# Upward products as 64-row halves on both row tiles, two units at a time, in a fused attention and channel-mix kernel

## The chip, the cores and the metric

The kernel runs on one core of one Trainium2 chip. The metric is the device time of one execution in microseconds (us); each time below is of this one core.

## What is computed

Two operators, one after the other, on x of shape 4 x 12608 x 128 (batch, tokens, channels), all in float32:

```python
# 1: attention through 32 inducing points; m = 32, C = 128, scale = C ** -0.5
def mab(q, kv):
    s = scale * (q @ kv.transpose(0, 2, 1)); s = s - s.max(-1, keepdims=True)
    a = np.exp(s); a /= a.sum(-1, keepdims=True) + 1e-09
    return a @ kv
h = mab(I, x)          # 32 x 128 per batch
x = mab(x, h)          # every token attends to the 32 rows of h
# 2: channel mix with the token before; d_ff = 1024
xk = mu_k * x + (1 - mu_k) * x_prev
xr = mu_r * x + (1 - mu_r) * x_prev
k = np.maximum(xk @ w_k, 0); v = k * k @ w_v
out = sigmoid(xr @ w_r) * v
```

The second attention's result is a product of weights `a` (tokens x 32) with `h`. So xk @ w_k is a[t] @ (h * mu_k @ w_k) + a[t-1] @ (h * (1 - mu_k) @ w_k): the kernel never forms x again, it multiplies the 32 weights of a token and of the token before with two small matrices W that it makes once per batch.

## The kernel before

**Tiling.** A batch has 25 groups of tokens: 24 of 512 (G) and a last one of 320. A block is four groups, so a batch has seven blocks, the last with the 320 tokens alone. d_ff is 1024 = 8 chunks of 128; a *unit* is one group with two chunks (UC = 2), four units to a group, so 100 units to a batch and 400 in all.

**A unit.** `up` (L774) makes the products of two chunks in PSUM, `square` (L786) has VectorE take the maximum with 0 (L792) and ScalarE square it twice, once rounded to fp32r (kh, L797; in some units VectorE does that, L794) and once in full (L798); GpSimd takes the difference kl (L800). `down` (L803) multiplies kh and kl with the high and low parts of w_v, six matmuls into one PSUM bank, four units after the unit's `up` (LAG = 4). Once in four units `zgate` (L761) makes the gate: two matmuls (L769, L770) and a sigmoid (L772). `gate` and `store` finish a group.

**Split numbers.** A matmul takes fp32r, a rounded float32. So the weights `a` are kept as a high and a low part. The tile R of a group, 128 rows x 513, holds in its four strips of 32 rows high, low, high, low; W[0] (this token, mu_k) and W[1] (the token before) hold in theirs high, high, low, low. One 128-row matmul thus gives all four cross products, and the token before is the same R one column to the left. That makes four 128-row matmuls in an `up`: for each of two chunks W[0] with R[:, 1:w+1] (L780) and W[1] with R[:, 0:w] (L782).

**Where R and W come from.** `stage_b` (L599) makes the weights of a block in steps at due times t to t+9 and `spread` (L663) puts one group a unit, from t+10 on, into R with four DMAs on SP's queue, and one more (`halo`, L589) for the column of the token before. For the first four groups `stage_b_head` (L688) does it with transposes on TensorE and one ScalarE copy (L745). `combine` (L473) makes h and W: scaled copies of h (L515), products with w_k and w_r, high on ScalarE, low on VectorE; for the first batch eight full products L538 with L541 and L544, for the others packs of four in the column strips (L556) and then 24 DMAs (L572) that spread the strips into W.

**The order of the work** is written out by hand: in the loop over units n (from L1017) each engine's queue gets, in this order, `gate` of a group that is done, `up(n)`, `square(n)`, GpSimd's difference, `zgate` if the unit is the second of its group, `store`, `down(n-4)`, and then the events whose due time is n. `stage_a` (first attention of the next batch, L313) and `stage_b` put their steps into this table at due times counted in units, 12 units to a block (SEG), from the offset t = 100 b (plus 4 for the first batch, L996). The engines then run their queues in order and wait for one another by semaphores. `spin` (L889) is a short burst of TensorE work in the head whose results nobody reads.

PSUM has eight banks: ps_a two tiles of two banks (the `up` products), ps_v two, pb_a and pb_b one each. So `up(n)` waits until VectorE has read `up(n-2)`.

Of the kernel before, what the change touches and what calls it, by code (L numbers as in the profile page):

```python
# [8 lines left out]
F32 = mybir.dt.float32  # L9
# [10 lines left out]
def kernel(  # L20
# [24 lines left out]
    LAG = 4  # L45
    UO = 2
# [10 lines left out]
    r_pool = ctx.enter_context(tc.tile_pool(name="r_pool", bufs=10))  # L57
# [415 lines left out]
    def combine(b, at=None, t=0):  # L473
# [18 lines left out]
        def weights():  # L492
# [11 lines left out]
            sw = sm.tile([P, P], F32, name="mk", bufs=1)  # L504
            if ahead:
                nc.vector.tensor_scalar(out=sw, in0=stack_f, scalar1=wt, scalar2=rd,
                                        op0=ALU.mult, op1=ALU.mult)
            else:
                nc.vector.tensor_scalar(out=sw, in0=stack_f, scalar1=rd, scalar2=None, op0=ALU.mult)
            L["sw"] = sw  # L510

        def mixed(*parts):
            for nm, mu in parts:
                h4 = L["h4"][nm] = sm.tile([P, P], F32, name="h4" + nm, bufs=1)
                nc.vector.tensor_scalar(out=h4, in0=L["hp"], scalar1=mu, scalar2=None, op0=ALU.mult)  # L515

        def hfin():
            ps = pb_tile(None if ahead else "b")
            nc.tensor.matmul(out=ps[:, :P], lhsT=S.acc, rhs=L["sw"], start=True, stop=True)
            h = sm.tile([P, P], F32, name="hT")  # L520
            nc.vector.tensor_copy(out=h, in_=ps[:, :P])
            S.hT = h[:, :M]
            L["hp"] = ps[:, :P]
            L["h4"] = {}
            mixed(("k0", muk), ("k1", omuk))
            mixed(("r0", mur), ("r1", omur))
            S.W = [wp.tile([P, WF], F32R, name=f"W{s}") for s in range(2)]

        def wpart(s, c, tile):

            X = {}
            c0, cw, nm, src = ((F, C, f"r{s}", wr_sb) if c is None else
                               (c * G, G, f"k{s}", wk_sb[:, c * G:(c + 1) * G]))
            dst = S.W[s][:, c0:c0 + cw]

            def prod():
                X["ps"] = tile()[:, :cw]
                nc.tensor.matmul(out=X["ps"], lhsT=L["h4"][nm], rhs=src, start=True, stop=True)  # L538

            def high():  # L540
                nc.scalar.copy(out=dst, in_=X["ps"])  # L541

            def low():
                nc.vector.tensor_tensor(out=dst[P // 2:], in0=X["ps"][P // 2:, :],  # L544
                                        in1=dst.bitcast(F32)[P // 2:], op=ALU.subtract)
            return prod, high, low

        def wpack(parts, cw, tags, t):

            X = {}  # L550
            rows = M * len(parts)

            def prod():
                X["ps"] = pb_tile("a")
                for n, (s, nm, c0, src) in enumerate(parts):
                    nc.tensor.matmul(out=X["ps"][M * n:M * (n + 1), :cw], lhsT=L["h4"][nm][:, :M], rhs=src,  # L556
                                     start=True, stop=True)

            def high():
                X["hi"] = st.tile([P, G], F32R, name=tags[0], bufs=tags[2])[:rows, :cw]  # L560
                nc.scalar.copy(out=X["hi"], in_=X["ps"][:rows, :cw])

            def low():
                lo = st.tile([P, G], F32R, name=tags[1], bufs=tags[2])[:rows, :cw]
                hi = X["hi"].bitcast(F32)
                nc.vector.tensor_tensor(out=lo, in0=X["ps"][:rows, :cw], in1=hi, op=ALU.subtract)
                X["hl"] = (hi, lo.bitcast(F32))

            def spread(n):
                s, nm, c0, src = parts[n]  # L570
                for q in range(Q):
                    nc.sync.dma_start(out=S.W[s].bitcast(F32)[M * q:M * (q + 1), c0:c0 + cw],  # L572
                                      in_=X["hl"][q // 2][M * n:M * (n + 1)])
            at(t, prod)
            at(t, high)
            at(t + 1, low)
            for n in range(len(parts)):
                at(t + 1 + n, lambda n=n: spread(n))
# [5 lines left out]
        parts = [(s, f"k{s}", c * G, wk_sb[:, c * G:(c + 1) * G]) for c in range(F // G) for s in range(2)]  # L584
        for n in range(0, len(parts), Q):
            wpack(parts[n:n + Q], G, ("ah", "al", 1), t + 11 + 4 * (n // Q))
        wpack([(s, f"r{s}", F, wr_sb) for s in range(2)], C, ("xs", "xs", 3), t + 13)

    def halo(S, g, far=True):  # L589

        if g == 0:
            nc.vector.memset(S.R[g].bitcast(F32)[:, 0:1], 0.0)
        elif far:
            nc.sync.dma_start(out=S.R[g].bitcast(F32)[:, 0:1], in_=S.R[g - 1].bitcast(F32)[:, G:G + 1])
        else:
            nc.vector.tensor_copy(out=S.R[g][:, 0:1], in_=S.R[g - 1].bitcast(F32)[:, G:G + 1])


    def stage_b(b, j, at, t):  # L599
# [55 lines left out]
        def high():  # L655
            L["ah"] = st.tile([P, G], F32R, name="ah")[:, :w]
            nc.scalar.copy(out=L["ah"], in_=L["aT"])

        def low():
            L["al"] = st.tile([P, G], F32R, name="al")[:, :w]  # L660
            nc.vector.tensor_tensor(out=L["al"], in0=L["aT"], in1=L["ah"].bitcast(F32), op=ALU.subtract)

        def spread(i):  # L663
            src = (L["ah"].bitcast(F32), L["al"].bitcast(F32))
            if full or i == 0:
                S.R[j * Q + i] = r_pool.tile([P, G + 1], F32R, name="R")
                halo(S, j * Q + i)
            R = S.R[j * Q + (i if full else 0)].bitcast(F32)
            o, lo = (0, 0) if full else (offs[i], i * w - offs[i])
            for q in range(Q):  # L670
                nc.sync.dma_start(out=R[M * q:M * (q + 1), 1 + o + lo:1 + o + w],
                                  in_=src[q % 2][M * i:M * (i + 1), lo:w])
# [12 lines left out]
        for i in range(Q):  # L685
            at(t + 10 + i, lambda i=i: spread(i))

    def stage_b_head(gs):  # L688
# [7 lines left out]
        def scores():  # L696
            ps = L["ps"] = pb_tile("b")
            for k, g in enumerate(gs):
# [5 lines left out]
                S.R[g] = r_pool.tile([P, G + 1], F32R, name="R")  # L704

        def diff():
            s2 = L["s2"] = st.tile([P, Q * Q, M], F32, name="s2")[:, :n, :]
# [16 lines left out]
        def place(k):  # L724
            g = gs[k]
            X = {}

            def src():
                return L["s2"][:, k * Q:(k + 1) * Q, :].unsqueeze(2).broadcast_to([P, Q, 2, M])

            def high():
                X["a"] = st.tile([P, G], F32R, name=("ah", "al")[g % 2]) \
                    .rearrange("p (k q m) -> p k q m", k=Q, q=Q)
                nc.scalar.copy(out=X["a"][:, :, 0::2, :], in_=src())

            def low():
# [110 lines left out]
    def halves():  # L847

        for name in ("kh", "kl"):
            for _ in range(4):  # L850
                yield mp.tile([P, UC, G], F32, name=name, bufs=4)
# [228 lines left out]
```

## Time and profile before

| what | value |
|---|---|
| median of 3 runs | 1146.32 us (1145.34 to 1148.07) |
| profiled execution | 1144.99 us, its span 1142.9 us, granted TensorE clock 0.993 |
| busy: PE, DVE, ACT, POOL | 1103.4, 917.7, 971.3, 948.4 us |
| instructions | 17673 |
| DMA | 102.32 MB in 274988 packets |

PE is TensorE's matmuls, PEld its weight loads, DVE VectorE, ACT ScalarE, POOL GpSimd, SP the engine whose queue issues nearly all DMAs. Busy time of PE is a union of spans: matmuls are pipelined, a matmul of 512 columns is drawn about 0.39 us long while the next one starts 0.23 us after it. So pace is read from starts, not from lengths. A row of the timeline gives the start, the time that the merged instructions cover, the engine, the line, tiles and shape (`64*128 64x512` is a stationary operand of 64 rows and 128 columns, and 64 rows x 512 columns that move), and in brackets the idle time before and what ended it.

### The profile page before, as it was taken

The page shows a single profiled execution, that of the slowest core. Times are in us where ns is not written, and L with a number is a line of the kernel's source. Part 1 is how long each engine was busy: PE and PEld are TensorE (multiplying, and loading weights), DVE is VectorE, ACT ScalarE, POOL GpSimd, SP SyncE. Part 2 cuts the span into 40 slices and gives each one's busy share as a digit, 9 for nine tenths or more (in the row PEclk, how much of TensorE's full clock was granted, in tenths as well). Part 3 has the DMA queues.
Part 4 walks back from the last instruction along what each step waited for, and adds up shares of the span by engine and source line. Part 5 has one row for each costly group of instructions (what it writes and reads, how often), then busy time and mean ns, then how long its engine had stood idle before and what let it go on. Part 6 is the DMA issues. An engine that isn't in the chain of part 4 may idle for free.

```text
span 1142.9 us, 17673 instructions
## 1 busy us (share of the span) xinstructions
PE 1103.4 (97%) x5716; PEld 837.4 (73%) x5716; DVE 917.7 (80%) x1294; ACT 971.3 (85%) x1107; POOL 948.4 (83%) x413
## 2 busy tenths in 40 slices
PE   6778999999989999999999999999999999999997
PEld 4456777777777777777877777777778777777886
DVE  5687898987678889897777889898777888887665
ACT  5477889888988888888988988889889988889996
POOL 1157888998887988888889888888888899999996
PEclk9999999999999999999999999999999999999999
DMA  9213444555135455555124455545222233242212
GB/s 275 69 28 91 106 108 111 129 127 108 31 70 119 91 121 124 125 124 124 24 61 87 110 128 120 129 99 124 50 50 61 46 64 59 54 74 56 43 28 34
DMA packets 274988, 102.32 MB, mean 90 GB/s; under 512 B 234288, under 2 KB 249808, under 8 KB 272592
## 3 DMA queue, kind: packets, MB, share of 16 engines
q1 hardware_dynamic: 274560, 101.18, 40.7%
q8 instruction: 45, 0.74, 0.3%
q14 instruction: 47, 0.39, 0.1%
q10 hardware_dynamic: 336, 0.02, 0.0%
HBM read 28.07 MB, written 25.82 MB: 47 GB/s over the span
## 4 chain that ended last, share of the span: by engine, by line
PE 79%; DVE 8%; ACT 7%; issue 3%; SPq 2%; DMA 1%; DVEq 0%; ACTq 0%
PE ps_v L811 40%; PE ps_a L780 15%; PE ps_a L782 13%; DVE k_t L792 3%; PE pb_b L617 2%; PE ps_v L769 2%; PE ps_v L770 2%; PE pb_a L359 2%; ACT kh L797 2%; PE pb_a L428 2%; ACT L772 1%; ACT L634 1%; ACT k_t L798 1%; SPq L93 1%; DVE kh L794 1%
## 5 line engine op out<-in xcount | busy, mean ns | idle before, releaser
L800 POOL TENSOR_TENSOR kl<-k_t,kh 128x1024 fp32r<-128x1024 f32 (+2 forms) x400 | 939.6, 2377 | 154.1 <-ACT k_t L798 136.4
L792 DVE TENSOR_SCALAR k_t<-ps_a 128x1024 f32<-128x1024 f32 (+1 forms) x400 | 480.2, 1201 | 162.1 <-PE ps_a L782 147.0
L798 ACT ACTIVATE k_t<-k_t 128x1024 f32<-128x1024 f32 (+1 forms) x400 | 418.3, 1048 | 46.9 <-DVE kh L794 35.7
L797 ACT ACTIVATE kh<-k_t 128x1024 fp32r<-128x1024 f32 (+1 forms) x352 | 366.0, 1040 | 81.5 <-PE ps_v L811 45.0
L780 PE MATMUL ps_a<-R,W 128*128 128x512 f32 (+1 forms) x800 | 324.5, 406 | 8.9 <-DMA R<-al 4.8
L782 PE MATMUL ps_a<-R,W 128*128 128x512 f32 (+1 forms) x800 | 314.3, 393 | 0.0
L811 PE MATMUL ps_v<-kh,wvh 128*128 128x512 f32 (+1 forms) x800 | 249.8, 393 | 5.3 <-ACT rT L772 4.7
L811 PE MATMUL ps_v<-kh,wvl 128*128 128x512 f32 (+1 forms) x800 | 249.3, 393 | 0.0
L811 PE MATMUL ps_v<-kl,wvh 128*128 128x512 f32 (+1 forms) x800 | 249.1, 392 | 0.1
L780 PEld LDWEIGHTS ps_a<-R,W 128*128 128x128 f32 x800 | 151.4, 189 | 82.9 <-issue 19.9
L811 PEld LDWEIGHTS ps_v<-kh,wvh 128*128 128x128 f32 x800 | 149.4, 189 | 44.0 <-ACT rT L772 10.0
L811 PEld LDWEIGHTS ps_v<-kl,wvh 128*128 128x128 f32 x800 | 150.3, 189 | 34.8 <-POOL kl L800 0.4
L811 PEld LDWEIGHTS ps_v<-kh,wvl 128*128 128x128 f32 x800 | 150.4, 189 | 34.1
L782 PEld LDWEIGHTS ps_a<-R,W 128*128 128x128 f32 x800 | 151.3, 189 | 30.7
L816 DVE TENSOR_TENSOR oT<-ps_v,rT 128x512 f32<-128x512 f32 (+1 forms) x100 | 66.7, 667 | 2.3
L827 DVE STREAM_TRANSPOSE ot<-oT 128x512 f32<-128x512 f32 x96 | 67.2, 700 | 0.0
L794 DVE SCALAR_TENSOR_TENSOR kh<-ps_a,k_t 128x1024 fp32r<-128x1024 f32 x48 | 58.8, 1225 | 5.4 <-DVE k_t L792 0.5
L772 ACT ACTIVATE rT<-ps_v 128x512 f32<-128x512 f32 (+1 forms) x99 | 57.3, 579 | 0.3
L331 DVE STREAM_TRANSPOSE xs<-xb 128x512 f32<-128x512 f32 x72 | 50.0, 694 | 2.5 <-DMA xt<-xs 1.2
L772 ACT ACT_TABLE_LOAD x31 | 39.8, 1283 | 0.5
L769 PE MATMUL ps_v<-R,W 128*128 128x512 f32 (+1 forms) x99 | 39.2, 396 | 0.8 <-DVE oT L816 0.8
L770 PE MATMUL ps_v<-R,W 128*128 128x512 f32 (+1 forms) x99 | 38.9, 393 | 0.0
(196 smaller groups left out, 614.8 us busy)
## 6 DMA issues: line engine op xcount, KB each, us to landing
out_dram<-ot SPq DMA_DIRECT2D x184, 128.0 KB, 3.3
xb<-in_x_dram SPq DMA_DIRECT2D x18, 1024.0 KB, 5.6
xt<-xs SPq DMA_DIRECT2D x288, 64.0 KB, 2.0
R<-ah SPq DMA_DIRECT2D x184, 64.0 KB, 2.0
R<-al SPq DMA_DIRECT2D x184, 64.0 KB, 2.0
kh<-in_x_dram SPq DMA_DIRECT2D x4, 512.0 KB, 7.3
kl<-in_x_dram SPq DMA_DIRECT2D x4, 512.0 KB, 7.5
xb<-in_x_dram SPq DMA_DIRECT2D x8, 256.0 KB, 5.8
```

The lines of the kernel that those rows point to most:

```text
L769: nc.tensor.matmul(out=ps[:, :w], lhsT=S.W[0][:, F:WF], rhs=R[:, 1:w + 1], start=True, stop=False)
L772: nc.scalar.activation(out=self.rT, in_=ps[:, :w], func=AF.Sigmoid)
L780: nc.tensor.matmul(out=ps[:, c, :w], lhsT=S.W[0][:, cs], rhs=R[:, 1:w + 1], start=True, stop=False)
L782: nc.tensor.matmul(out=ps[:, c, :w], lhsT=S.W[1][:, cs], rhs=R[:, 0:w], start=False, stop=True)
L792: nc.vector.tensor_scalar(out=k, in0=self.ps[:, :, :w], scalar1=0.0, scalar2=None, op0=ALU.max)
L794: nc.vector.scalar_tensor_tensor(out=kh, in0=self.ps[:, :, :w], scalar=0.0, in1=k, op0=ALU.max, op1=ALU.mult)
L797: nc.scalar.activation(out=kh, in_=k, func=AF.Square)
L798: nc.scalar.activation(out=k, in_=k, func=AF.Square)
L800: return lambda eng, a, z: eng.tensor_tensor(out=kl[:, :, a:z], in0=k[:, :, a:z], in1=kh.bitcast(F32)[:, :, a:z], op=ALU.subtract)
L811: nc.tensor.matmul(out=self.v, lhsT=wt[:, fc, :], rhs=kk[:, c, :], start=(fc == 0 and n == 0), stop=(fc == FC - 1 and n == 2))
L816: nc.vector.tensor_tensor(out=self.oT, in0=self.v, in1=self.rT, op=ALU.mult)
L827: nc.vector.transpose(out=ot[:, o:o + w], in_=self.oT)
```

## The change

It has these parts:

- `up` keeps the chunks but changes the products (new constants: HP = 64, NR = 5). R now has 64 rows that matter: 0 to 31 the token's weights, 32 to 63 those of the token before, and rows 64 to 127 the same again; its second index says high or low. W[0] (high) and W[1] (low) hold in rows 0 to 63 the even chunks (this token over the token before), in rows 64 to 127 the odd ones. A unit is then three products (W high x R high, W low x R high, W high x R low; low x low is left out), each as two matmuls of 64 rows, one on each row tile of the array, into two PSUM banks.
- `up(n)` and `up(n+1)` are issued one after the other, at even n; both `down`s follow later as before, as whole matmuls of 128 rows.
- `zgate` still has two whole matmuls, now with one matrix Wg of 128 rows against R high and R low.
- W is made by one pack of four products whose strips lie already as W needs them: one ScalarE copy, one VectorE difference, no DMA. Wg likewise.
- R is filled by two DMAs (the token's rows, and the same one column on), a small one for the first column, and two units later by one DMA of 64 rows x 2 x 512 (`double`) that copies rows 0 to 63 to 64 to 127. R has 5 buffers instead of 10, and a fill is due no earlier than the last unit of the group five before.
- The first four groups: eight transposes of 32 columns a group; for group 0 four ScalarE and four VectorE copies, for the others one of each and `double`.
- kh has 5 buffers instead of 4; the first batch's offset in the table of due times is 1 instead of 4.

```diff
-    r_pool = ctx.enter_context(tc.tile_pool(name="r_pool", bufs=10))
+    r_pool = ctx.enter_context(tc.tile_pool(name="r_pool", bufs=NR))
...
         def hfin():
-            nc.tensor.matmul(out=ps[:, :P], lhsT=S.acc, rhs=L["sw"], start=True, stop=True)
+            nc.tensor.matmul(out=ps[:, :M], lhsT=S.acc, rhs=L["sw"], start=True, stop=True)
...
+            h4 = L["h4"] = sm.tile([P, Q, M], F32, name="h4", bufs=1)
+            for n, mu in enumerate((muk, omuk, mur, omur)):
+                nc.vector.tensor_scalar(out=h4[:, n, :], in0=ps[:, :M], scalar1=mu, scalar2=None, op0=ALU.mult)
+            S.W = [wp.tile([P, F // 2], F32R, name=f"W{s}") for s in range(2)]
+            S.Wg = wp.tile([P, C], F32R, name="Wg")
...
             def prod():
                 X["ps"] = tile()[:, :cw]
+                chunks = wk_sb.rearrange("p (c e d) -> p e c d", e=2, d=P)
+                for n in range(Q):
+                    o = X["ps"][M * n:M * (n + 1), :]
+                    if not gate:
+                        o = o.rearrange("m (c d) -> m c d", d=P)
+                    nc.tensor.matmul(out=o, lhsT=L["h4"][:, 2 * gate + n % 2, :],
+                                     rhs=wr_sb if gate else chunks[:, n // 2], start=True, stop=True)
             def high():
+                nc.scalar.copy(out=(S.Wg if gate else S.W[0]), in_=X["ps"])
             def low():
+                hi, lo = (S.Wg, S.Wg) if gate else S.W
+                nc.vector.tensor_tensor(out=lo[rows], in0=X["ps"][rows], in1=hi.bitcast(F32)[rows],
+                                        op=ALU.subtract)
...
+        for gate in range(2):
+            prod, high, low = wpart(gate, lambda: pb_tile("a"))
+            at(t + 11 + 2 * gate, prod)
+            at(t + 11 + 2 * gate, high)
+            at(t + 12 + 2 * gate, low)
...
+    def new_r(S, g, src=None):
+        R = S.R[g] = r_pool.tile([P, 2, G], F32R, name="R")
...
+        nc.sync.dma_start(out=rf[M:HP, :, 0:1], in_=src[:, :, G - 1:G])
+    def double(S, g):
+        rf = S.R[g].bitcast(F32)
+        w = G if g < NG - 1 else TAIL
+        nc.sync.dma_start(out=rf[HP:, :, :w], in_=rf[:HP, :, :w])
+    def fill(rf, src, o, n, width):
+        for s in range(2):
+            m = min(n, width - o - s)
+            nc.sync.dma_start(out=rf[M * s:M * (s + 1), :, o + s:o + s + m], in_=src[:, :, :m])
...
         for i in range(Q):
-            at(t + 10 + i, lambda i=i: spread(i))
+            f = b * NG + j * Q + (i if full else 0)
+            s = max(t + 10 + i, NU * (f - NR) + 3 + (0 if full else i))
+            at(s, lambda i=i: spread(i) if full else spread_tail(i))
+            assert s + 4 <= NU * f, (b, j, i)
+            if full or i == Q - 1:
+                at(s + 2, lambda g=j * Q + i if full else j * Q: double(S, g))
...
+        def put(k, whole):
             g = gs[k]
+            ps = pa.tile([P, 2, G], F32, name="ps_a")
+            for s in range(2):
                 for c in range(Q):
+                    nc.tensor.transpose(out=ps[:M, s, c * P:(c + 1) * P], identity=ident,
+                                        in_=L["a"].bitcast(F32)[:, k * Q + c, s, :])
...
+            if not whole:
+                nc.scalar.copy(out=R[:M], in_=ps[:M])
+                nc.vector.tensor_copy(out=R[M:HP, :, 1:], in_=ps[:M, :, :G - 1])
+                return
...
+            for s in range(2):
+                for r in range(2):
+                    nc.scalar.copy(out=R[HP * r:HP * r + M, s], in_=ps[:M, s])
+                    nc.vector.tensor_copy(out=R[HP * r + M:HP * (r + 1), s, 1:], in_=ps[:M, s, :G - 1])
...
-            for c in range(UC):
-                cs = slice((u * UC + c) * P, (u * UC + c + 1) * P)
-                nc.tensor.matmul(out=ps[:, c, :w], lhsT=S.W[0][:, cs], rhs=R[:, 1:w + 1],
-                                 start=True, stop=False)
-                nc.tensor.matmul(out=ps[:, c, :w], lhsT=S.W[1][:, cs], rhs=R[:, 0:w],
-                                 start=False, stop=True)
+            for n, (a, k) in enumerate(((0, 0), (1, 0), (0, 1))):
+                for r in range(2):
+                    rows = slice(HP * r, HP * (r + 1))
+                    nc.tensor.matmul(out=ps[:, r, :w], lhsT=S.W[a][rows, u * P:(u + 1) * P],
+                                     rhs=R[rows, k, :w], start=(n == 0), stop=(n == 2))
...
-        t = b * UB + (4 if b == 0 else 0)
+        t = b * UB + (1 if b == 0 else 0)
...
-                grp.up(u)
+                if n % 2 == 0:
+                    for g, v in units[n:n + 2]:
+                        g.up(v)
```

More of the change, by code (lines that the diff above doesn't have):

```diff
@@ L45 @@
     LAG = 4
+    HP = P // 2
+    NR = 5
     UO = 2
@@ L546, in wpart @@
             return prod, high, low
[L548 to L578, printed above, removed]
@@ L655, in high, with spread_tail @@
         def high():
-            L["ah"] = st.tile([P, G], F32R, name="ah")[:, :w]
-            nc.scalar.copy(out=L["ah"], in_=L["aT"])
+            if full:
+                L["hl"] = st.tile([P, 2, G], F32R, name="hl", bufs=2)
+            else:
+                L["hl"] = st.tile([P, G], F32R, name="xs", bufs=3)[:, :2 * w].rearrange("p (s t) -> p s t", s=2)
+            nc.scalar.copy(out=L["hl"][:, 0, :], in_=L["aT"])
         def low():
-            L["al"] = st.tile([P, G], F32R, name="al")[:, :w]
-            nc.vector.tensor_tensor(out=L["al"], in0=L["aT"], in1=L["ah"].bitcast(F32), op=ALU.subtract)
+            nc.vector.tensor_tensor(out=L["hl"][:, 1, :], in0=L["aT"], in1=L["hl"].bitcast(F32)[:, 0, :],
+                                    op=ALU.subtract)
         def spread(i):
[L664 to L672, printed above, removed]
+            hl = L["hl"].bitcast(F32)
+            g = j * Q + i
+            src = hl[M * i:M * (i + 1)]
+            rf = new_r(S, g, hl[M * (i - 1):M * i] if i else None)
+            fill(rf, src, 0, G, G)
+        def spread_tail(k):
+            g = j * Q
+            rf = new_r(S, g) if k == 0 else S.R[g].bitcast(F32)
+            lo = k * w - offs[k]
+            fill(rf, L["hl"].bitcast(F32)[M * k:M * (k + 1), :, lo:], k * w, w - lo, TAIL)
         at(t, scores)
@@ L748, in stage_b_head, with high, low @@
-        return scores, diff, expo, norm, [place(k) for k in range(len(gs))]
+        def high():
+            a = L["a"] = st.tile([P, 2, G], F32R, name="hl", bufs=2) \
+                .rearrange("p s t -> p (s t)")[:, :2 * n * M].rearrange("p (k s m) -> p k s m", s=2, m=M)
+            nc.scalar.copy(out=a[:, :, 0, :], in_=L["s2"])
+        def low():
+            nc.vector.tensor_tensor(out=L["a"][:, :, 1, :], in0=L["s2"], in1=L["a"].bitcast(F32)[:, :, 0, :],
+                                    op=ALU.subtract)
@@ L751 @@
+        return scores, diff, expo, norm, high, low, put
     NG = (NBLK - 1) * Q + 1
@@ L768, in zgate @@
                 ps = self.v = pv.tile([P, G], F32, name="ps_v")[:, :w]
-            nc.tensor.matmul(out=ps[:, :w], lhsT=S.W[0][:, F:WF], rhs=R[:, 1:w + 1], start=True, stop=False)
-            nc.tensor.matmul(out=ps[:, :w], lhsT=S.W[1][:, F:WF], rhs=R[:, 0:w], start=False, stop=True)
+            for s in range(2):
+                nc.tensor.matmul(out=ps[:, :w], lhsT=S.Wg, rhs=R[:, s, :w], start=(s == 0), stop=(s == 1))
             self.rT = mp.tile([P, G], F32, name="rT")[:, :w]
```

130 lines of the change are left out of this document (38 added, 92 removed).

## The prediction

> **What bounds the kernel now.** I read the page first: the shares of the engines, the chain of work that ended last, and the costliest groups.
>
> ```profile
> span 1142.9 us, 17673 instructions
> PE 1103.4 (97%) x5716; PEld 837.4 (73%) x5716; DVE 917.7 (80%) x1294; ACT 971.3 (85%) x1107; POOL 948.4 (83%) x413
> PE 79%; DVE 8%; ACT 7%; issue 3%; SPq 2%; DMA 1%; DVEq 0%; ACTq 0%
> L800 POOL TENSOR_TENSOR kl<-k_t,kh 128x1024 fp32r<-128x1024 f32 (+2 forms) x400 | 939.6, 2377 | 154.1 <-ACT k_t L798 136.4
> L792 DVE TENSOR_SCALAR k_t<-ps_a 128x1024 f32<-128x1024 f32 (+1 forms) x400 | 480.2, 1201 | 162.1 <-PE ps_a L782 147.0
> ```
>
> TensorE is busy for 97% and makes 79% of the chain; VectorE's main step waits 147 us in all for the upward products. But an average over stages hides two limits, so I asked for the busy times of each stage: middle of the first batch, second batch, the last batch up to its last 25 units, and those.
>
> ```profile
> core 0: us, PE busy (x) PEld busy (x) DVE busy (x) ACT busy (x) POOL busy (x), PEclk, DMA share, GB/s
> 137.00:206.00 69.00, 69.00 (x366) 50.81 (x365) 62.32 (x88) 60.59 (x68) 60.56 (x26) 1.00 0.49 106
> 342.00:613.00 271.00, 269.59 (x1380) 203.59 (x1380) 225.48 (x319) 236.22 (x263) 232.15 (x99) 0.99 0.46 100
> 883.00:1075.00 192.00, 190.57 (x842) 148.44 (x842) 153.85 (x179) 172.35 (x182) 177.81 (x77) 1.00 0.31 57
> 1075.00:1132.00 57.00, 57.00 (x253) 46.53 (x252) 36.94 (x37) 51.68 (x54) 57.00 (x26) 1.00 0.21 33
> ```
>
> In the first three batches TensorE has no idle time while ScalarE, GpSimd and VectorE are at 83 to 90%: a unit takes 2.7 us (271 us for 100) and TensorE sets it. In the last batch GpSimd is at 93%, and in the last 25 units at 100%: there nothing taken from TensorE shows, because L800 alone needs 2.4 us a unit. So the change can pay in about 375 units, and only what it takes off TensorE's pace.
>
> **The change, step by step.** The pace first, from the starts of one undisturbed unit (ten matmuls lie from the first row to the last):
>
> ```profile
> 91.90 0.39 PE L780 MATMUL ps_a<-R,W 128*128 128x512 f32 x1
> ...
> 94.22 0.40 PE L780 MATMUL ps_a<-R,W 128*128 128x512 f32 x1
> ```
>
> 2.32 us for ten: 0.232 us each. The change takes the eight whole matmuls out of two units (1.86 us) and puts in twelve halves. The head happens to run just such halves, in `spin`: whole matmuls, eight halves on both row tiles, whole ones again, with nothing to wait for between.
>
> ```profile
> 45.34 0.40 PE L895 MATMUL ps_a<-wvh 128*128 128x512 f32 x1
> 45.66 0.77 PEld L899 LDWEIGHTS ps_a<-wvh 64*128 64x128 f32 x8 [0.36 <-issue]
> 46.01 0.85 PE L899 MATMUL ps_a<-wvh 64*128 64x512 f32 x5
> 46.47 0.41 PE L899 MATMUL ps_a<-wvh 64*128 64x512 f32 x2
> 47.14 0.40 PE L902 MATMUL ps_a<-wvh 128*128 128x512 f32 x1
> ```
>
> The rows are the last whole matmul, the weight loads of the halves, the second pair onward, the last pair, and the second whole matmul after. From the second pair to the fourth is 0.46 us, 0.23 us a pair: two halves cost what one whole does, each with its own weights. Twelve halves are then 6 x 0.23 = 1.38 us, and two units save 0.46 to 0.48; I take a pair at the pace of a whole matmul, so two slots, 2 x 0.232 = 0.464 us. But from the last whole to the second pair are two steps that take 0.67 instead of 0.46 us, and from the last pair to the second whole again 0.67: each change of the tiling costs 0.21 us, half before the first matmul of the new kind and half behind it. I take 0.205. Two units change into halves and back: 0.41 us. So the net is 0.464 - 0.41 = 0.054 us for two units. The Trainium skill, TensorEngine Tiling (Array Packing), section Key Properties, states that changing the tiling mode drains TensorE; the trace agrees, with 0.21 us for each change.
>
> Over the run: 200 pairs x 0.464 = 92.8 us out, 400 changes x 0.205 = 82 us in. Some of these are not new, for `stage_a`, `stage_b` and W already put blocks of 128*32 matmuls between whole ones:
>
> ```profile
> 99.74 0.63 PE L811 MATMUL ps_v<-kl,wvh 128*128 128x512 f32 x2
> 100.31 1.06 PE L359 MATMUL pb_a<-xt,indT 128*32 128x512 f32 x8
> 101.30 0.50 PE L780 MATMUL ps_a<-R,W 128*128 128x512 f32 x1
> 101.64 0.39 PE L782 MATMUL ps_a<-R,W 128*128 128x512 f32 x1
> ```
>
> L359 starts 0.57 us after the first of two matmuls that need 0.464, so 0.11 late, and the second matmul behind the block comes 0.34 instead of 0.23 us after the first: the same price as in `spin`, here with real waits. A block that is due in an odd unit now lies between whole and half products: one new change instead of two. By the due times of the changed code these are 6 of L428 and 1 of L617 in the first batch, 6 of L359, 6 of L617 and 2 that make W in each of the next two, 6 of L617 in the last: 41 x 0.205 = 8.4 us back. So TensorE gains 92.8 - 82 + 8.4 = 19.2 us, of which about 0.8 (13 pairs of the last 25 units) is hidden behind GpSimd.
>
> **PSUM.** The second `up` of a pair now waits for the read of the unit before it with no `down` ahead. Queued behind it on TensorE are both `down`s, the gate and the stage blocks.
>
> ```profile
> 90.77 1.23 DVE L792 TENSOR_SCALAR k_t<-ps_a 128x1024 f32<-128x1024 f32 x1 [0.21 <-PE ps_a L782]
> ...
> 93.09 1.22 DVE L792 TENSOR_SCALAR k_t<-ps_a 128x1024 f32<-128x1024 f32 x1
> L624 DVE STREAM_TRANSPOSE s<-pb_b 128x512 f32<-128x512 f32 x23 | 16.2, 705 | 0.0
> ```
>
> The read of 90.77 ends at 92.00, and the `up` that needs its bank starts at 94.22: 2.2 us of room. The second `up` moves ahead by six `down` matmuls, 1.39 us, so 0.8 us is left. Steps of the stages such as L624 (0.7 us) come between the reads, two at times; nothing in this trace shows such a wait, so it costs from 0 up to some 0.6 us in three units of each of 24 blocks, 40 us. I take 4 us, near the lower end, because its data also come earlier.
>
> **R and W.** `double` is a second DMA behind the first. In steady state it is due 15 units before its reader, and SP's queue is not full. What matters is where R was late or close.
>
> ```profile
> 108.71 0.47 PE L780 MATMUL ps_a<-R,W 128*128 128x512 f32 x1 [2.48 <-DMA R<-al]
> 340.42 0.46 PE L780 MATMUL ps_a<-R,W 128*128 128x512 f32 x1 [2.33 <-DMA R<-al]
> 602.46 0.78 SPq L671 DMA_DIRECT2D R<-ah  x1
> 612.31 0.40 PE L780 MATMUL ps_a<-R,W 128*128 128x512 f32 x1
> R<-ah SPq DMA_DIRECT2D x184, 64.0 KB, 2.0
> out_dram<-ot SPq DMA_DIRECT2D x184, 128.0 KB, 3.3
> xb<-in_x_dram SPq DMA_DIRECT2D x8, 256.0 KB, 5.8
> ```
>
> The first block's fill is due at unit 11 instead of 15 and is needed at 16: even with `double` the 2.48 us wait goes (-2.5, at worst +1). At 340 the first batch's three units of earlier offset (8 us) pay for `double` (two units later, 5.4 us, and 2.0 to 5.8 us to land, by the rows of 64 and 256 KB; I take 3.3): the wait stays about the same. At 612 the fill is issued 10 us before its reader: two units and 3.3 us make 8.7, just enough. For the three borders I take +1 us, from -2 to +6. The waits that SP gains lie before transfers with units of room. The 24 DMAs of W go, off the path.
>
> **Head.** Four scaled copies of 32 instead of 128 columns and one difference of W instead of four before the loop gain; the four ScalarE and four VectorE copies of group 0 lose.
>
> ```profile
> L745 ACT CAST R<-pb_a 128x512 fp32r<-128x512 f32 x4 | 2.3, 585 | 1.3 <-PE pb_a L743 1.3
> L544 DVE TENSOR_TENSOR W<-ps_v,W 64x512 fp32r<-64x512 f32 x4 | 2.8, 695 | 1.3 <-ACT W L541 1.2
> L515 DVE TENSOR_SCALAR h4k<-pb_b,muk 128x128 f32<-128x128 f32 x4 | 1.4, 343 | 0.0
> ```
>
> By these rows at most three more copies stand before the first `up` (3 x 0.6 to 0.7 = +2), against one or two differences (0.7 each) and most of four times 0.34: 0, from -3 to +3.
>
> Sum: -19.2 + 0.8 + 4 - 2.5 + 1 + 0 = -15.9 us. The profiled execution took 1144.99 us (span 1142.9 and 2.1 around it), 1.3 below the median of the runs; against the median that is 1146.3 - 15.9 = 1130.4, and I say 1130.
>
> **Rivals.**
> 1. *The second `up` waits (slower).* Mechanism as above: TensorE stands before the bank that VectorE has not read, with the `down`s behind it. For it: VectorE at 90% in 137 to 206, and always in the order of the program. Against it: the 0.8 us of room. Without my 4 us the sum is -19.9, so it decides from 0.1 us a pair (200 pairs); at 0.2 us in the 150 pairs of the first three batches it is -19.9 + 30 = +10, and with the borders at +6 instead of +1 it is +15: 1156 to 1161.
> 2. *The change of tiling costs more in the loop than in `spin` (slower).* 359 changes are new (400 - 41), so 92.8/359 = 0.258 us each makes nothing of the gain, and 0.3 makes +15 us: 1161. The block at 100.31 speaks against it.
> 3. *ScalarE and GpSimd set the pace (no change or a little faster).* They are at 86 to 88% in the second batch; if two reads in a row make them wait in turns, half or all of 16 us stays away: 1138 to 1147.
> 4. *The halves do not overlap.* If a weight load of 64 rows could not lie under the matmuls of its own tile, a pair would cost 0.23 plus a load of about 0.19 (the eight loads above cover 0.77 us in four pairs), six pairs 2.5 us: 200 x (2.5 + 0.41 - 1.86) = +210 us, 1356. The Trainium skill, TensorE: Matmul & The Clock Gate, Part 3, says that weight loads overlap with running matmuls only where their row groups differ, which would do this. `spin` contradicts it: its pairs follow at 0.23 us with new weights each.
>
> **Chances and range.** Forecast 0.62 (1118 to 1143); rival 1 0.16, rival 2 0.07, rival 3 0.12, rival 4 0.03. About 0.2% is what a measurement of this kernel can tell from no change, here 2.3 us. Faster: the forecast and half of rival 3, 0.68; same: the rest of it and its borders, 0.08; slower: the others, 0.24. The range leaves out rival 4, the worst of 1 and 2, and the ends of the forecast: 1115 to 1157.
>
> **What would show it.** Right: rows of `up` as 64*128 64x512, 2400 of them, pairs 0.23 us apart; 0.33 us from the last `down` to the first half, and 0.33 back; a unit at 2.64 to 2.67 us in the second batch with TensorE still without idle time; no wait for R before unit 16; the last 25 units still at 57 us. Wrong: idle time of TensorE before the halves ended by L792 (rival 1); starts of 0.4 us or more at the changes (rival 2); TensorE idle before `down`, ended by GpSimd, or VectorE waiting for k_t (rival 3); pairs 0.4 us apart (rival 4).

## The result, and the profile after it

The changed kernel takes 1160.59 us (median of 4 runs, 1158.34 to 1162.16) against 1146.28 before (4 runs): a ratio of 1.0121, 95% interval 1.0101 to 1.0142. It is slower, and outside the range of the prediction. Its profiled execution took 1160.58 us, with a span of 1158.8 and a mean granted TensorE clock of 0.974 (before: 0.993).

The page of the kernel after, with the lines that answer to those shown before; the second row is the granted clock in 40 slices of 29 us.

```profile
span 1158.8 us, 19210 instructions
PE 1089.2 (94%) x6548; PEld 740.6 (64%) x6548; DVE 919.0 (79%) x1293; ACT 976.2 (84%) x1112; POOL 945.2 (82%) x413
PEclk9869999989999989999999989999999999999999
...
PE 74%; DVE 9%; ACT 4%; DMA 4%; SPq 3%; POOL 3%; issue 2%; DVEq 0%; ACTq 0%; POOLq 0%
...
L792 DVE TENSOR_SCALAR k_t<-ps_a 128x1024 f32<-128x1024 f32 (+1 forms) x400 | 477.9, 1198 | 115.7 <-PE ps_a L782 85.4
...
R<-R SPq DMA_DIRECT2D x95, 256.0 KB, 3.1
```

TensorE is busy for 14 us less than before, in a span that is 16 us longer: it stands idle 30 us more. DMA and SP's queue now make 7% of the chain that ended last, 3% before. The clock row has dips that tell where.

The busy times by stage of the kernel before, cut at the start of VectorE's maximum (L792) of units 0, 25, 75, 100, 125, 200, 300 and 399 (two stretches left out):

```profile
core 0: us, PE busy (x) PEld busy (x) DVE busy (x) ACT busy (x) POOL busy (x), PEclk, DMA share, GB/s
61.10:136.90 75.80, 68.11 (x333) 50.88 (x333) 64.48 (x86) 61.93 (x71) 56.00 (x24) 0.95 0.35 83
136.90:274.30 137.40, 137.40 (x737) 102.33 (x736) 121.77 (x178) 120.24 (x135) 121.20 (x51) 1.00 0.52 117
...
341.70:410.10 68.40, 67.07 (x328) 50.58 (x327) 60.01 (x82) 57.18 (x61) 57.55 (x25) 0.98 0.52 116
410.10:613.50 203.40, 203.32 (x1059) 153.74 (x1058) 166.27 (x238) 179.51 (x204) 175.39 (x75) 1.00 0.44 95
...
883.00:1131.90 248.90, 247.47 (x1092) 194.88 (x1092) 190.70 (x215) 224.03 (x236) 234.71 (x102) 1.00 0.29 52
```

The same of the kernel after:

```profile
63.20:157.50 94.30, 76.69 (x415) 47.51 (x411) 67.62 (x91) 64.08 (x69) 58.39 (x25) 0.90 0.39 90
157.50:303.90 146.40, 136.47 (x814) 88.77 (x815) 119.97 (x175) 126.47 (x138) 114.67 (x49) 0.97 0.60 131
...
368.60:440.60 72.00, 66.82 (x377) 45.33 (x374) 60.21 (x83) 58.10 (x63) 59.86 (x27) 0.95 0.58 129
440.60:636.50 195.90, 195.71 (x1214) 134.36 (x1214) 165.86 (x238) 178.28 (x203) 174.91 (x75) 1.00 0.56 120
...
903.60:1148.20 244.60, 242.29 (x1302) 171.10 (x1298) 193.07 (x216) 221.95 (x238) 235.23 (x102) 1.00 0.40 74
```

In the order of the rows: the loop starts 2.1 us later (63.2 against 61.1), units 0 to 25 take 18.5 us more, units 25 to 75 take 9.0 more, units 100 to 125 take 3.6 more (the border to the second batch), units 125 to 200 take **7.5 less**, and the last batch 4.3 less. So the steady part gained what was forecast and more; the first batch and the borders gave back more than that. In the first batch TensorE is idle for 17.6 and 9.9 us of the two stretches, at a mean clock of 0.90 and 0.97.

What TensorE waited for, by the waits of the kernel after (us in total, times, longest):

```profile
PE ps_a L782 <- DVE k_t L792: 13.2, 9, 5.1
PE ps_a L782 <- DMA R<-R: 13.1, 4, 4.5
PE ps_a L782 <- DVE kh L794: 7.8, 6, 1.6
```

Three waits of the upward halves make 34 us. The first and the third are waits for a bank of PSUM that VectorE has not read; the second is for `double`, the copy of R's rows. TensorE's timeline of after shows a pair of units without a wait, the longest wait, and then one of each kind:

```profile
500.74 1.67 PE L782 MATMUL ps_a<-R,W 64*128 64x512 f32 x12
502.34 0.73 PE L811 MATMUL ps_v<-kh,wvh 128*128 128x512 f32 x2
...
82.31 1.65 PE L782 MATMUL ps_a<-R,W 64*128 64x512 f32 x6 [5.14 <-DVE k_t L792]
...
155.33 0.97 PE L782 MATMUL ps_a<-R,W 64*128 64x512 f32 x6
158.77 0.97 PE L782 MATMUL ps_a<-R,W 64*128 64x512 f32 x6 [2.47 <-DVE k_t L792]
...
183.81 0.97 PE L782 MATMUL ps_a<-R,W 64*128 64x512 f32 x6 [1.54 <-DVE kh L794]
...
412.67 1.65 PE L782 MATMUL ps_a<-R,W 64*128 64x512 f32 x6 [4.41 <-DMA R<-R]
```

At 500.74 twelve halves and one change of tiling take 1.60 us to the first `down`: 6 x 0.232 + 0.205 is 1.597. At 155.33 and 183.81 only six halves are issued; the other six, the second unit of the pair, wait. VectorE's timeline of after at the same places says why:

```profile
78.10 2.32 DVE L715 TENSOR_SCALAR sm<-sm 128x8 f32<-128x8 f32 x1
...
81.04 1.22 DVE L792 TENSOR_SCALAR k_t<-ps_a 128x1024 f32<-128x1024 f32 x1
...
156.89 0.71 DVE L333 STREAM_TRANSPOSE xs<-xb 128x512 f32<-128x512 f32 x1 [2.60 <-DMA xb<-in_x_dram]
157.53 1.19 DVE L792 TENSOR_SCALAR k_t<-ps_a 128x1024 f32<-128x1024 f32 x1
...
181.23 1.20 DVE L792 TENSOR_SCALAR k_t<-ps_a 128x1024 f32<-128x1024 f32 x1
182.53 1.23 DVE L794 SCALAR_TENSOR_TENSOR kh<-ps_a,k_t 128x1024 fp32r<-128x1024 f32 x1
...
89.45 1.21 DVE L739 CAST R<-ps_a 32x1022 fp32r<-32x1022 f32 x1 [3.95 <-ACT R L738]
...
99.20 1.21 DVE L739 CAST R<-ps_a 32x1022 fp32r<-32x1022 f32 x1 [3.79 <-ACT R L738]
```

Four causes, all ahead of a read of PSUM in VectorE's order: a load of x that comes late (at 231.32 again, by 3.99 us); a second read of the same bank (L794, which makes kh in two units of a block); and, in the first units, the copy L739 into R, which waits for ScalarE's copy L738 into the same tile. The fourth is behind the longest wait, 5.14 us at 82.31: seven steps of the stages stand between the two reads of that pair, from 75.72 to 81.04, and one of them, L715, took 2.32 us where it took 0.17 at 53.82. Why it took so long is not shown. SP's queue of after shows the late transfers:

```profile
218.87 2.65 SPq L834 DMA_DIRECT2D out_dram<-ot  x4
...
222.53 0.81 SPq L206 DMA_DIRECT2D xb<-in_x_dram  x1
...
405.78 3.02 SPq L834 DMA_DIRECT2D out_dram<-ot  x4
408.85 0.84 SPq L577 DMA_DIRECT2D R<-R  x1
```

The x load for which VectorE stands until 231.32 is issued behind the four stores of a group, which wait for VectorE's last step of that group; from its issue to 231.32 are 8.8 us, where the median to landing of these loads is 5.9. `double` for unit 116, needed at 408.26, is issued at 408.85, behind four stores too, whose issue alone takes 3.02 us there (SP is busy with transfers of xt up to 405.7, so here the queue's length counts more than a wait). The Trainium skill, DMA: Bandwidth & Descriptors, section Anatomy of one DMA — SWDGE (gpsimd) path, states that DMA engines do not wait on semaphores and that the issuing sequencer waits before it dispatches. That section is about transfers that GpSimd issues; for SP's queue the rows here agree, with transfers that need nothing from the stores held behind them for about 3 us.

The theory after this profile: TensorE's own terms were right, and what cost the time are waits outside the steady state: (A) the second `up` waits for PSUM in the first batch because of where its steps fall; (B) `double` is late in SP's queue; (C) the head's copies of R. The rivals: the halves or the changes of tiling cost more than they save, or two `up`s in a row wait for PSUM wherever they are.

### The profile page after: what moved, and what is told of

Read it like the earlier page. It is cut to its first block, busy times and chain, and to the rows that moved or that the text cites. A ratio compares the mean times of both kernels' runs of the same rounds, so it can differ in the third digit from the quotient of the medians.

```text
span 1158.8 us, 19210 instructions
## 1 busy us (share of the span) xinstructions
PE 1089.2 (94%) x6548; PEld 740.6 (64%) x6548; DVE 919.0 (79%) x1293; ACT 976.2 (84%) x1112; POOL 945.2 (82%) x413
## 4 chain that ended last, share of the span: by engine, by line
PE 74%; DVE 9%; ACT 4%; DMA 4%; SPq 3%; POOL 3%; issue 2%; DVEq 0%; ACTq 0%; POOLq 0%
PE ps_v L811 41%; PE ps_a L782 23%; DVE k_t L792 4%; PE ps_v L770 3%; POOL kl L800 3%; PE pb_b L603 2%; DMA R<-R 2%; PE pb_a L361 1%; PE pb_a L430 1%; SPq L834 1%; ACT k_t L798 1%; DVE kh L794 1%; DMA xb<-in_x_dram 1%; SPq L95 1%; DMA kl<-in_x_dram 1%
## 5 line engine op out<-in xcount | busy, mean ns | idle before, releaser
L792 DVE TENSOR_SCALAR k_t<-ps_a 128x1024 f32<-128x1024 f32 (+1 forms) x400 | 477.9, 1198 | 115.7 <-PE ps_a L782 85.4
L782 PE MATMUL ps_a<-R,W 64*128 64x512 f32 (+1 forms) x2400 | 344.7, 414 | 37.6 <-DVE k_t L792 13.2
L782 PEld LDWEIGHTS ps_a<-R,W 64*128 64x128 f32 x2400 | 212.0, 187 | 167.9 <-issue 51.5
L811 PE MATMUL ps_v<-kh,wvh 128*128 128x512 f32 (+1 forms) x800 | 273.9, 424 | 1.0 <-ACT rT L772 0.9
L811 PEld LDWEIGHTS ps_v<-kh,wvh 128*128 128x128 f32 x800 | 133.3, 190 | 98.9 <-issue 42.5
L816 DVE TENSOR_TENSOR oT<-ps_v,rT 128x512 f32<-128x512 f32 (+1 forms) x100 | 67.1, 671 | 17.1 <-PE ps_v L811 16.3
L770 PE MATMUL ps_v<-R,Wg 128*128 128x512 f32 (+1 forms) x198 | 61.2, 390 | 0.0
L794 DVE SCALAR_TENSOR_TENSOR kh<-ps_a,k_t 128x1024 fp32r<-128x1024 f32 x48 | 58.8, 1225 | 2.4
L333 DVE STREAM_TRANSPOSE xs<-xb 128x512 f32<-128x512 f32 x72 | 49.9, 694 | 7.0 <-DMA xb<-in_x_dram 6.6
L770 PEld LDWEIGHTS ps_v<-R,Wg 128*128 128x128 f32 x198 | 37.3, 189 | 9.1 <-DVE k_t L792 0.8
L603 PE MATMUL pb_b<-xt,hT 128*32 128x512 f32 x184 | 25.9, 637 | 3.6 <-DVE aT L703 3.6
L364 DVE TENSOR_REDUCE mx<-pb_a 128x1 f32<-128x512 f32 x18 | 12.5, 692 | 16.7 <-PE pb_a L361 16.7
```

What stands on the lines that cost most here:

```text
L333: nc.vector.transpose(out=xs.rearrange("p (s q) -> p s q", q=M), in_=S.xb[j][:, :, M * c:M * (c + 1)])
L770: nc.tensor.matmul(out=ps[:, :w], lhsT=S.Wg, rhs=R[:, s, :w], start=(s == 0), stop=(s == 1))
L782: nc.tensor.matmul(out=ps[:, r, :w], lhsT=S.W[a][rows, u * P:(u + 1) * P], rhs=R[rows, k, :w], start=(n == 0), stop=(n == 2))
L792: nc.vector.tensor_scalar(out=k, in0=ps, scalar1=0.0, scalar2=None, op0=ALU.max)
L794: nc.vector.scalar_tensor_tensor(out=kh, in0=ps, scalar=0.0, in1=k, op0=ALU.max, op1=ALU.mult)
L811: nc.tensor.matmul(out=self.v, lhsT=wt[:, fc, :], rhs=kk[:, c, :], start=(fc == 0 and n == 0), stop=(fc == FC - 1 and n == 2))
```

## The experiments

Each is an edit of the kernel after. Ratios are against the kernel before on the same chip (median 1143 to 1146 us), with their 95% intervals. The time of 25 or 50 units is taken between the same maxima as above.

**e1_even.** The double reads of the first batch go to even units.

```diff
-            high_vector |= {s + 4, s + 8}
+            high_vector |= {s + 4 + s % 2, s + 8 + s % 2}
```

> One line: in the first batch the units in which VectorE reads PSUM twice (L792 and L794) move from odd to even units, where the other batches have them. Theory A (the second upward product of a pair waits for VectorE's reads of the unit before, and that decides only where the double read falls on the odd unit): the waits of 1.4 to 3.9 us at 145, 159, 184, 218, 233 and 259 us go, 12 us, and with them two stretches at half the clock; 1160.6 becomes 1149 to 1153. Rival B (the odd offset of the first batch's whole table is to blame, or pairs in general): the waits move to other units and the time stays within 3 us.

1154.40 us, 1.0084 (1.0065 to 1.0103). Units 25 to 75:

```profile
152.20:295.90 143.70, 134.94 (x814) 87.95 (x815) 119.93 (x176) 126.65 (x138) 115.67 (x49) 0.98 0.60 133
```

143.7 instead of 146.4 us, with the waits behind L794 gone and the two behind late loads of x left (1.51 and 3.51 us on VectorE). The three waits of 1.54 to 1.57 us behind L794 in these units are replaced rather than gone: each of their pairs now has two shorter waits, such as 0.81 us at 173.12 (the gate's matmuls, for VectorE's L816) and 0.56 us at 176.71 (the second `up`, for L792), 1.37 to 1.42 us together. So rival B is right in part, waits move; the double reads alone are a small part of A.

**e2_double.** `double` is due one unit after its fill instead of two.

```diff
-                at(s + 2, lambda g=j * Q + i if full else j * Q: double(S, g))
+                at(s + 1, lambda g=j * Q + i if full else j * Q: double(S, g))
```

> One number: the copy of rows 0-63 of R to rows 64-127 is put into SP's queue one unit after the fill instead of two. Theory A (the copy is late because it stands in SP's queue behind four stores of the output that wait for VectorE, though its data landed 9 us before): the waits for R at 127, 413, 681 and 943 us (13.1 us together) and the half-clock stretches behind two of them go; 1160.6 becomes 1140 to 1148. Rival B (the second transfer in a row is itself too slow): the waits shrink by less than half, 1154 or more. Rival C: SP now stands before each copy until the fill has landed, which holds up the transfers of the first attention, and the time does not fall.

1151.23 us, 1.0063 (1.0041 to 1.0085). Of the waits for R<-R in the loop, one of 0.19 us (at 76.36) is left. Units 100 to 125, which took 72.00 us:

```profile
363.20:431.60 68.40, 65.46 (x377) 43.49 (x374) 59.87 (x83) 57.81 (x63) 59.79 (x27) 1.00 0.66 142
```

As long as before the change. Cause B is shown, and one unit of due time cures it. But the time is above the 1140 to 1148 expected, and there are waits that the change did not have, as the expectation's rival C said. VectorE stands 2.53 us for a transfer of xt (L333 at 374.25), and TensorE then 1.64 us for VectorE at 375.99, and 2.08 us at 642.18. That the earlier `double` holds up SP's queue there is likely, and was not tried apart.

**e3_put.** In the head, VectorE's copy L739 goes to ScalarE, and in group 0 the two engines copy opposite halves.

```diff
-                nc.vector.tensor_copy(out=R[M:HP, :, 1:], in_=ps[:M, :, :G - 1])
+                nc.scalar.copy(out=R[M:HP, :, 1:], in_=ps[:M, :, :G - 1])
...
+                    v = 1 - s
-                    nc.vector.tensor_copy(out=R[HP * r + M:HP * (r + 1), s, 1:], in_=ps[:M, s, :G - 1])
+                    nc.vector.tensor_copy(out=R[HP * r + M:HP * (r + 1), v, 1:], in_=ps[:M, v, :G - 1])
```

> The copies that make R of the first four groups no longer alternate between ScalarE and VectorE on the same columns: groups 1 to 3 have both copies on ScalarE, group 0 has ScalarE and VectorE on different halves at a time. Theory A (VectorE stands 2.5 to 4 us before each such copy until ScalarE has done its own, and the next unit's reads and the upward products stand behind it): the first 25 units take 94.3 us now and then 82 to 87, the time 1148 to 1153. Rival B (the ramp is long because the stages start three units earlier and VectorE has too much to do): the 25 units stay above 91 us and the time within 4 us of 1160.6.

1151.61 us, 1.0061 (1.0042 to 1.0080). Units 0 to 25:

```profile
64.00:148.70 84.70, 74.88 (x413) 47.76 (x411) 65.00 (x89) 66.75 (x72) 58.53 (x25) 0.90 0.44 100
```

84.7 instead of 94.3 us: C is shown for the copies of groups 1 to 3. For group 0 the crossing failed: the engines still took turns, and TensorE waited 4.0 us for them until 60.98. They read different banks then, so it isn't one bank that orders them; whether it is the tile R or the whole tile of PSUM was not tried apart.

**e4_single** and **e5_whole** measure TensorE's terms. e4 issues each unit's `up` alone, still as halves, so that there is a change of tiling into and out of each unit:

```diff
-                if n % 2 == 0:
-                    for g, v in units[n:n + 2]:
-                        g.up(v)
+                grp.up(u)
```

> The upward products of each unit are issued alone, still as halves: the number of changes of tiling doubles and nothing waits at the second product of a pair. Theory A (a change costs 0.2 us, pairs hide half of them): 200 more changes in and out, 82 us of TensorE, less some waits: 1215 to 1240. Rival B (the pairs' waits for PSUM are what the change loses by): 1160 or less.

e5 keeps the order in pairs and issues four whole products of 128 rows, which do not form the reference's sums:

```diff
-            for n, (a, k) in enumerate(((0, 0), (1, 0), (0, 1))):
-                for r in range(2):
-                    rows = slice(HP * r, HP * (r + 1))
-                    nc.tensor.matmul(out=ps[:, r, :w], lhsT=S.W[a][rows, u * P:(u + 1) * P],
-                                     rhs=R[rows, k, :w], start=(n == 0), stop=(n == 2))
+            for r in range(2):
+                for n in range(2):
+                    nc.tensor.matmul(out=ps[:, r, :w], lhsT=S.W[n][:, u * P:(u + 1) * P],
+                                     rhs=R[:, n, :w], start=(n == 0), stop=(n == 1))
```

> The order of the changed kernel with two units in a row, its tiles and its DMAs, but each unit's upward products are four whole 128-row matmuls again (W high by R high and W low by R low over all rows, which sums two chunks into one and leaves out W low by R high and W high by R low: the values are not the reference's, the work is that of the kernel before). It takes the halves alone out of the change. Theory A (halves save 0.46 us a pair and cost two changes of tiling, 0.41 us, less where a block of the stages lies beside them; the loss lies in waits that order, table and DMAs bring): a unit in the middle of the second batch takes 2.75 to 2.80 us again instead of 2.56 to 2.69, the waits for R and in the ramp stay, the time is 1170 to 1185. Rival B (the halves and their changes of tiling are the loss): the time falls under 1150.

e4: 1208.35 us, 1.0553 (1.0537 to 1.0569). e5: 1168.84 us, 1.0214 (1.0192 to 1.0235). Units 125 to 175, in all three with TensorE without idle time; first the kernel after:

```profile
440.60:571.80 131.20, 131.20 (x826) 89.01 (x825) 119.44 (x174) 118.03 (x133) 118.05 (x50) 1.00 0.66 147
```

The same windows view of e4:

```profile
438.80:580.80 142.00, 142.00 (x831) 86.64 (x832) 121.02 (x173) 119.53 (x135) 120.08 (x51) 1.00 0.61 136
```

And of e5:

```profile
443.10:576.80 133.70, 133.70 (x726) 101.51 (x725) 119.47 (x174) 118.16 (x133) 118.35 (x50) 1.00 0.64 145
```

The two further changes for two units in e4 cost 10.8 us in 50 units, 0.43 for two units; `spin` had given 2 x 0.205 = 0.41. Halves save 2.5 us in 50 units against whole products, 0.050 a unit; the prediction had 19.2/400 = 0.048. The rival that the halves or the changes cost more than they save falls.

**e6_all.** e1 and e2 together, and all copies of R in the head on ScalarE (for group 0 four of 32 rows x 1024):

```diff
+            for r in range(2):
+                nc.scalar.copy(out=R[HP * r:HP * r + M], in_=ps[:M])
+                nc.scalar.copy(out=R[HP * r + M:HP * (r + 1), :, 1:], in_=ps[:M, :, :G - 1])
```

> The three edits together: double reads of PSUM on even units, the copy of R one unit after its fill, all copies of R in the head on ScalarE (for group 0 four of 32x1024 instead of eight alternating ones). Theory A (three separate causes): the single gains of 6.2, 9.4 and 9.0 us add up, 1160.6 to 1134 to 1139, faster than the kernel before by 0.6 to 1%. Rival B (they cover each other: what one frees the next wait takes): 1143 or more.

1140.95 us (12 runs), 0.9966 (0.9954 to 0.9977): faster than before. By the ratios the three single gains add up (0.0037, 0.0058 and 0.0060 from 1.0121 give 0.9966), so the causes are separate; the 1134 to 1139 had been added up from times on different chips. But units 25 to 75 still took 144.8 us: a part of cause (A) was left, so the next edits took the offset itself, which is 1 in the change and was 4 before.

**e7_offset2, e9_offset3, e10_offset0.** The first batch's steps are due 2, 3 or 0 units after its start instead of 1; to keep the last block of the batch in time, e7 and e9 let one `stage_b` start one or two units earlier, and e10 lets events due before unit 0 run at it.

```diff
-        t = b * UB + (1 if b == 0 else 0)
+        t = b * UB + (2 if b == 0 else 0)
...
-            stage_b(b + 1, 0, at, s + 13)
+            stage_b(b + 1, 0, at, s + (12 if b == 0 else 13))
```

> The first batch's offset in the table of due times is 2 instead of 1, so that all steps of the stages fall on units of the same parity as in the other batches; the first step for the second batch is one unit nearer so that its R is due as before. Theory A (what stands between the two reads of a pair decides: with an odd offset the heavy VectorE steps lie between them): units 25 to 75 take 2.6 to 2.75 us instead of 3.07 and 2.79, the time is 1147 to 1152. Rival B (only the double reads matter): as with these alone moved, 1153 to 1156. Rival C (the first batch is slow for another reason): 1158 or more.

> The changed kernel with offset 3 for the first batch instead of 1, the first step for the second batch two units nearer so that R is due as before. Nothing else differs. Theory A (parity: with an odd offset the double reads and the heavy steps of VectorE fall between the two reads of a pair): units 25 to 75 as slow as with offset 1 (2.9 to 3.1 and 2.7 to 2.8 us), the time 1152 to 1162, though the ramp is a little shorter. Rival B (a later table is simply better for the ramp): 1142.6, as with offset 2, or less.

> The changed kernel with offset 0 for the first batch instead of 1 (what would be due before unit 0 is due at unit 0). Theory A (parity): units 25 to 75 as with offset 2 (2.9 and 2.6 us), the time 1142 to 1151, a longer ramp included. Rival B (later is better): 1160 or more.

| offset | us | ratio | units 25 to 75 | VectorE waits for x | double reads fall on |
|---|---|---|---|---|---|
| 0 (e10) | 1139.51 | 0.9953 (0.9939 to 0.9968) | 131.2 us | none | even units |
| 1 (the change) | 1160.59 | 1.0121 (1.0101 to 1.0142) | 146.4 | 2.60 + 3.99 | odd |
| 2 (e7) | 1142.57 | 0.9973 (0.9959 to 0.9988) | 137.9 | 5.53 | even |
| 3 (e9) | 1152.10 | 1.0061 (1.0039 to 1.0084) | 140.0 | none | odd |

The windows of units 25 to 75, first of e7:

```profile
145.60:283.50 137.90, 134.11 (x827) 90.40 (x826) 121.00 (x180) 117.96 (x133) 118.38 (x51) 0.99 0.64 141
```

Of e9:

```profile
156.10:296.10 140.00, 136.56 (x833) 89.33 (x832) 121.48 (x180) 118.11 (x132) 118.99 (x50) 1.00 0.63 142
```

Of e10, with the second batch's units 125 to 175 in the second row:

```profile
151.50:282.70 131.20, 131.20 (x826) 89.15 (x825) 119.46 (x174) 118.03 (x133) 118.08 (x50) 1.00 0.66 148
418.60:549.80 131.20, 131.20 (x825) 89.14 (x825) 119.44 (x175) 117.73 (x133) 117.77 (x50) 1.00 0.66 147
```

With offset 0 the first batch runs like the second, to the tenth of a microsecond, and TensorE has no idle time in it. The table separates two effects: against offset 0, odd steps alone (offset 3) cost 8.8 us in these 50 units, a late load alone (offset 2) costs 6.7, both (offset 1) 15.2, near their sum. (Some work also moves across the end of the stretch with the offset; by units 75 to 100, 64.7, 63.2 and 64.2 us for offsets 0, 3 and 2, that is at most 1.5 us.) Since e1 gained only 2.7 us, the double reads are not all of the odd part; the shorter steps that fall between the two reads of a pair were not taken apart. The rival that two `up`s in a row wait for PSUM wherever they are falls: with even steps they do not.

The waits of e10 show what is left:

```profile
PE ps_a L782 <- DMA R<-R: 16.2, 5, 5.0
...
PE ps_a L782 <- DVE k_t L792: 3.0, 6, 1.5
```

**e8_all_offset2, e11_all_offset0.** Offset 2 or 0, with `double` one unit after its fill and the head's copies on ScalarE as in e6.

> Offset 2, the copy of R one unit after its fill, and the head's copies of R on ScalarE. Theory A: the waits of the first batch between units 25 and 75 go as well, 3 to 8 us below the three edits with the odd offset: 1128 to 1134. Rival B: the parity of the other steps does not matter, the same as the three edits with the odd offset within 2 us.

> Offset 0, the copy of R one unit after its fill, the head's copies of R on ScalarE. Theory A (three separate causes add up): from 1139.5 with offset 0 alone, 13 to 18 us less, 1121 to 1127, below the 1128.9 with offset 2. Rival B (the x loads late in SP's queue take back what the earlier copy gives): 1128 or more.

e8: 1128.87 us, 0.9863 (0.9848 to 0.9877). e11: 1125.93 us (5 runs), 0.9846 (0.9824 to 0.9869), the lowest of all, though its interval overlaps that of e8. Both are faster than the kernel before and the changed kernel. The page of e11:

```profile
span 1123.2 us, 19261 instructions
...
PE 1074.1 (96%) x6548; PEld 737.0 (66%) x6548; DVE 913.5 (81%) x1286; ACT 967.0 (86%) x1105; POOL 945.8 (84%) x413
```

Its windows of units 0 to 25 and 25 to 75:

```profile
63.70:141.70 78.00, 68.33 (x402) 44.89 (x401) 65.33 (x89) 62.45 (x69) 55.97 (x24) 0.94 0.48 109
141.70:272.90 131.20, 131.20 (x826) 88.95 (x825) 119.49 (x174) 117.94 (x133) 118.20 (x50) 1.00 0.67 148
```

The three cures add up: by the ratios the offset is worth 0.0168 (1.0121 to 0.9953), `double` 0.0058, the head's copies 0.0060, together 0.0286; e11 has 0.0275.

The causes came out much as the theories A said, the sizes often did not. The times of e3, e8, e9 and e11 lie in their expected ranges; e1, e2 and e6 gained less than expected; e4 (1215 to 1240 expected), e5 (1170 to 1185), e7 (1147 to 1152) and e10 (1142 to 1151) came out faster.

## Why the prediction was wrong

- **Pace, halves, change of tiling: right.** 1.60 us measured for twelve halves and a change against 1.597; from the last `down` to the first half the starts lie 0.33 us apart and 0.32 back (medians), forecast 0.33; 0.050 us a unit against 0.048 (e5); 0.43 us for two changes against 0.41 (e4). `spin`, a burst with nothing to wait for, was the right place to read a price for the loop. That blocks in odd units share a change was not tried by itself; the trace bears out the count, with a half right behind a 128*32 matmul 41 times, and 350 changes between whole and half products where the prediction counted 359.
- **PSUM: the step that failed.** It took 4 us, spread over "three units of each of 24 blocks" of the run, and argued with 0.8 us of room. The runs show about 20 us (1160.59 to 1139.51, e10), all in the first batch; in units 125 to 200 TensorE is busy for 195.71 of 195.90 us. Not all of it is parity: the wait of 5.14 us at 82.31 stays (5.14 and 5.17 us) with offsets 2 and 3, and is 1.46 us with offset 0. The room was read from one undisturbed pair of reads, while the question is which VectorE steps stand between the two reads of a pair. That depends on whether a step is due in an odd or an even unit, which the prediction did not ask, and on the loads that those steps wait for. The change also moves the first batch's offset from 4 to 1; the prediction used this for when R is filled, and not for what it does to the order on VectorE and SP. Rival 1 named this wait and gave 1156 to 1161; the time fell there, but with 0.2 us in each of 150 pairs, where it was 21 us in fifteen waits, beside the terms for R and the head that had failed too: its time was met by luck.
- **R and W: failed too.** "In steady state it is due 15 units before its reader, and SP's queue is not full" does not hold for the groups filled at the start of a batch: `double` then stands behind the transfers of xt and four stores. The prediction looked at the three borders, at units 100, 200 and 300; the waits were 16 units later, 2.90 us at unit 16 and 4.41, 4.51 and 1.25 us at units 116, 216 and 316. The wait of 2.48 us that was to go stayed as 2.90, and the one of 2.33 us at unit 100 that was to stay went. The prediction had -2.5 and +1 us here; e2 puts the late `double` at 0.0058 of the time, 6.6 us.
- **Head: failed in its scope.** The start of the loop moved by 2.1 us, inside the -3 to +3. But the copies for groups 1 to 3 run within the loop's first units, and their taking turns was no term of the sum; units 0 to 25 took 18.5 us more, of which `double` and the offset share a part, and in e11 still 2.2 us more. The prediction had 0 us here; e3 puts the copies at 0.0060, 6.9 us.
- **The last 25 units: right in what sets them, not in their length.** GpSimd is busy for 59.99 of 60.27 us from the maximum of unit 375 to that of unit 399. But this stretch was to stay as it was, and it took 58.16 us before. The last batch as a whole gained 4.3 us in 100 units where units 125 to 200 gained 7.5 in 75.
- **The steady part gained more than forecast.** 7.5 us in 75 units; halves are 3.3 of them (199.2 us in e5 against 195.9). The other 4.2 us lie in two places that the traces show. One block of the first attention waits for its xt in the kernel before, and takes 2.70 us from its start at 532.43 to the next product, where the block at 499.85 took 1.00. And whole matmuls start a little closer together: in these units the median from start to start is 232 ns for those of `down` and 235 ns for those of `up` in the kernel before, 229 ns for both in e5, and 230 ns for `down` in the changed kernel. Over some 790 whole matmuls that makes about 3 us, an estimate from these medians; why they follow faster stays open. The steady part also helps e11 to land at 1125.9, below the 1130 of the forecast; the shares were not taken apart.

## What to carry to other kernels

Price a change of order by asking, for each wait that it tightens, which instructions stand ahead of the releaser in each queue, in every stage and at every phase of the schedule, not by the room of one undisturbed case. Where work is issued in pairs, odd and even due times become different places: put long steps on the engine that frees the buffer outside the pair's reads. A transfer that somebody waits for belongs ahead of stores in its queue, since four stores hold up what is behind them by 3 us of issue, and longer where they wait for their data.

## What was not expected of the hardware

An idle stretch of TensorE can cost more than its length. The windows of after over an idle stretch of 2.47 us and what follows it, and over what follows waits of 4.41, 1.54 and 2.90 us:

```profile
156.30:158.77 2.47, 0.00 (x1) 0.00 (x1) 1.88 (x3) 0.00 (x0) 2.11 (x1) 1.00 0.04 12
159.80:163.20 3.40, 3.40 (x10) 1.81 (x14) 2.95 (x4) 3.22 (x5) 2.11 (x1) 0.50 0.48 106
...
412.67:419.20 6.53, 6.53 (x20) 4.74 (x21) 4.75 (x5) 2.20 (x3) 1.90 (x2) 0.50 0.74 163
...
183.80:190.60 6.80, 6.79 (x39) 3.97 (x40) 4.94 (x9) 6.54 (x8) 5.99 (x4) 1.00 0.27 100
...
127.01:133.80 6.79, 6.76 (x37) 4.58 (x37) 5.61 (x7) 4.33 (x6) 2.88 (x2) 1.00 0.64 144
```

After 2.47 us without a matmul the granted clock is 0.50 for 3.4 us and after 4.41 us for 6.5 us; after 1.54 us it stays at 1.00. The length alone does not decide: after the 2.90 us before unit 16 it stays at 1.00 too, though after 2.48 us in the kernel before it is 0.50 again, for 3.4 us from 109.64. At 0.50 whole matmuls start 0.43 us apart instead of 0.23. So a wait of 4.4 us can cost about 3.0 us more behind it (6.5 x (1 - 0.23/0.43), an estimate), which a list of waits does not count. The Trainium skill, TensorE: Matmul & The Clock Gate, section HAM oscillation — how this bites in real kernels, gives the rule as no idle gaps of TensorE over about 3.4 us; here 2.47 and 2.48 us were enough and 2.90 us was not, and the measurement decides.
